# Dealing the units of an inner layer to partitions in runs of 7 and 9

## The chip, the cores and the metric

The kernel runs on one core of a Trainium2 chip. A core has five engines that run side by side, each with its own queue of instructions: TensorE (PE; its weight loads are listed apart as PEld), VectorE (DVE), ScalarE (ACT), GpSimd (POOL) and SyncE (SP, which only issues transfers here). Transfers between the large memory (HBM) and the on-chip memory (SBUF, 128 partitions) are done by 16 DMA engines. TensorE multiplies a stationary operand, which it loads first (LDWEIGHTS, at most 128 columns), with a moving operand and adds into the accumulator memory (PSUM). The metric is the device time of one execution in microseconds (us); where several runs are shown, their median.

## The reference

Two layers follow one another. The first is a short convolution along the sequence whose 7 taps differ for every token and head; the second is a two-matrix layer applied to each of the 32768 tokens.

```python
# x [8, 4096, 192], weight_gen [8, 4096, 8 heads, 7 taps]
w = exp(weight_gen - max) / sum over the taps
conv[b, s, h, g] = sum over k of w[b, s, h, k] * x_padded[b, s + k, h, g]   # 6 zero rows ahead
# w_in [192, 2048], w_out [2048, 192]
h = conv @ w_in
g = h - tanh(h)
out = g @ w_out            # [32768, 192], float32
```

The 2048 columns of `w_in` are the units of the inner layer. The output is a sum over units, so it doesn't matter in which order the units are taken, so long as column u of `w_in` and row u of `w_out` stay together.

## The kernel before

The tokens are cut into 32 tiles (`n`) of 1024, 8 neighbouring tokens to a partition. For each tile:

- SP loads the tile's `x` and tap weights. ScalarE takes the exponential; VectorE sums over the taps and divides.
- GpSimd, with help from VectorE, multiplies x with each tap's weight (`tap_product`, L303). Some of the seven products are added to each other by transfers that accumulate, issued by GpSimd (`dma_sum`, L292).
- TensorE turns the remaining products so that features lie on the partitions, and adds them up while it does so (`conv_sums`, L531: each product is the stationary operand, the identity the moving one). The 192 features are split as 64 x 3 with the 3 innermost, so a stationary operand there takes every third column. The 64 features of a group lie on the lower half of the partitions for one half of the tokens and on the upper half for the other. ScalarE copies the result to SBUF as `convT`.
- First matmul (`gemm1`, L591): for each of 16 blocks `f` of 128 units, three feature groups, and on both halves of the partitions at once: stationary `w_in` [64 features x 128 units], moving `convT` [64 x 512 tokens]. So six matmuls a block, which are three pairs, each pair on the two halves of the rows. `w_in` is kept twice for this, on the lower and on the upper 64 partitions.
- ScalarE takes tanh of the block's result (L604), VectorE subtracts (L605) and writes `gt`, bf16, with the 128 units of the block on the partitions.
- Second matmul (`out_stream`, L660): for each of 8 groups of 128 tokens, over the 16 blocks and the two halves of the units: stationary `gt` [64 units x 128 tokens], moving `w_out` [64 units x 192]. ScalarE copies the sums out (L679) and SP stores them.

The order of all this is written out by hand (`manual_schedule`). In tile n's turn the main loop goes over the 16 blocks: it issues `gemm1(n, f)` and then a number of steps of the second matmul of the tile before, read from a table (`pairs`, one number for each block; a zero means that the next block of the first matmul follows directly). The transposes of the next tile come behind blocks 13 and 14 in most turns. The last tile's second matmul is `last_rows` (L709).

Partition p of `w_out` in SBUF holds, for each block f, the row of the unit that the first matmul puts on partition p in block f. Before the change that is unit f*128 + p, since `gemm1` takes 128 adjacent columns of `w_in`. The weights are loaded once, at the start, by GpSimd, with a conversion from float32 to bf16: `w_in` in two parts, columns 0 to 895 (seven blocks, `FA = 7 * P`) and columns 896 to 2047 (nine blocks), both at L755; `w_out` in one transfer at L749, issued between GpSimd's tap products of tile 1. The upper copy of `w_in` is made by ScalarE for the first part (L822) and by a transfer on SP for the second (L830). The variant of the first matmul at `gemm1_relieved` is for blocks in the list `RELIEF`, which is empty.

Of the kernel before, what the change touches and what calls it, by code (L numbers as in the profile page):

```python
# [16 lines left out]
def kernel(  # L17
# [8 lines left out]
    nc = tc.nc  # L26
# [5 lines left out]
    P = nc.NUM_PARTITIONS  # L32
    R = P // 2
# [8 lines left out]
    NFT = F // P  # L42
# [214 lines left out]
    def softmax_norm_ramp(n, bank):  # L257

        softmax_sum(n)
        wsm = softmax_tile()  # L260
        zr_v = bank[:, 512 - J * H : 512]
        nc.vector.reciprocal(zr_v, zsum_of[n][:])  # L262
        if n == 2:
            scale(nc.vector, wsm[:], e_of[n], zr_v)
            wsm_of[n] = (wsm, None, None, None)
            return
        wsm_v = bank[:, 0 : J * H * K].rearrange("p (j h k) -> p j h k", j=J, h=H)
        if RAMP_TAPS is not None:
            for to_sbuf, k0, k1 in RAMP_TAPS[n]:
                ramp_scale[n] = scale(nc.vector, wsm[:] if to_sbuf else wsm_v, e_of[n], zr_v, k0, k1)  # L270
            wsm_of[n] = (wsm, wsm_v, None, None)
            return
        if n == 0 and SCALE_TWICE:
            scale(nc.vector, wsm[:], e_of[n], zr_v)
        ramp_scale[n] = scale(nc.vector, wsm_v, e_of[n], zr_v)
        if n == 1 or not SCALE_TWICE:
            nc.scalar.activation(
                out=wsm[:].rearrange("p j h k -> p (j h k)"),
                in_=wsm_v.rearrange("p j h k -> p (j h k)"),
                func=ACT.Copy,  # L280
            )
        wsm_of[n] = (wsm, wsm_v, None, None)
# [286 lines left out]
    def gemm1(n, f):  # L569
        convT = conv_of[n]  # L570
        ph = psum_h.tile([P, 2, HT], FP32, name="ph", tag="ph")
        ff = slice(f * P, (f + 1) * P)
        if n in THREE:
            block = convT[:].rearrange("p c (a t) -> p (c a) t", t=P).rearrange("p (j b) t -> p b j t", b=NC)
            for r, b, c, p0, p1, last in (
                (0, 0, 0, 0, P, False),
                (1, 2, 1, 0, P, False),
                (0, 1, 2, 0, R, True),
                (1, 1, 2, R, P, True),
            ):  # L580
                nc.tensor.matmul(
                    ph[:, r, :],
                    lhsT=w_nat_of[0][p0:p1, c, ff],
                    rhs=block[p0:p1, b],
                    start=not last,
                    stop=last,
                )
        else:
            for c in range(NC):
                for r in range(2):  # L590
                    nc.tensor.matmul(  # L591
                        ph[:, r, :],
                        lhsT=w_in[r * R : (r + 1) * R, c, ff],
                        rhs=convT[r * R : (r + 1) * R, c, :],
                        start=(c == 0),
                        stop=(c == NC - 1),
                    )
        th = tpool.tile([P, TOK], FP32, name="th")
        ph_f = ph[:].rearrange("p r t -> p (r t)")
        gt = gpool.tile([P, TOK], BF16, name=f"gt{f}", tag=f"gt{f}")  # L600
        if n == 1 and f == 2:

            probe[0] = nc.scalar.activation(out=once[:], in_=ph_f[:, 0:1], func=ACT.Copy)
        last_act[0] = nc.scalar.activation(out=th[:], in_=ph_f, func=ACT.Tanh)  # L604
        last_sub[0] = nc.vector.tensor_sub(gt[:], ph_f, th[:])  # L605
        if f == PACE:
            pace_of[n] = last_sub[0]
        g_of.setdefault(n, []).append(gt)
        return ph

    def gemm1_relieved(n, f):

        convT = conv_of[n]
        for c in range(NC):
            for r in range(2):
                nc.tensor.matmul(
                    obank[r][:],
                    lhsT=w_in[r * R : (r + 1) * R, c, f * P : (f + 1) * P],
                    rhs=convT[r * R : (r + 1) * R, c, :],
                    start=(c == 0),  # L620
                    stop=(c == NC - 1),
                )
        th = tpool.tile([P, TOK], FP32, name="th")
        gt = gpool.tile([P, TOK], BF16, name=f"gt{f}", tag=f"gt{f}")
        for r in range(2):
            nc.scalar.activation(out=th[:, r * HT : (r + 1) * HT], in_=obank[r][:], func=ACT.Tanh)
        g_of.setdefault(n, []).append(gt)

        def subtract():
            for r in range(2):  # L630
                nc.tensor.matmul(
                    obank[r][:], lhsT=minus[:], rhs=th[:, r * HT : (r + 1) * HT], start=False, stop=True
                )

        def evict():
            for r in range(2):
                nc.scalar.activation(out=gt[:, r * HT : (r + 1) * HT], in_=obank[r][:], func=ACT.Copy)

        return subtract, evict
# [59 lines left out]
    def last_rows(r):  # L699

        n = NTOT - 1
        for j in range(J):
# [5 lines left out]
            for f in range(NFT):  # L708
# [17 lines left out]
                        )  # L726
                yield

    w_in = const.tile([P, NC, F], BF16, name="w_in")
    w_out = const.tile([P, NFT, D], BF16, name="w_out")  # L730
    w_nat_of = {}
# [14 lines left out]
    ctx.enter_context(tc.manual_schedule())  # L746

    def load_w_out():
        nc.gpsimd.dma_start(out=w_out[:], in_=moe_w_out.rearrange("(c p) e -> p c e", c=NFT))  # L749

    FA = 7 * P

    def load_w_in(c0, c1, f0, f1, behind=None):
        src = moe_w_in[c0 : c0 + 1, f0:f1]
        dma = nc.gpsimd.dma_start(  # L755
            out=w_in[0:R, c0:c1, f0:f1],
            in_=bass.AP(
                tensor=src.tensor,
                offset=src.offset,
                ap=[[NC * F, R], [F, c1 - c0], [1, f1 - f0]],  # L760
            ),
        )
        if behind is not None:
            order(dma, behind, "order of the loads")

    def rest_of_w_in():
        load_w_in(0, NC, FA, F)

# [9 lines left out]
    for c0, c1 in W_CUTS:  # L778
        load_w_in(c0, c1, 0, FA, last_exp[0] if c0 == 0 else None)
    softmax_norm_ramp(0, obank[0])  # L780
# [36 lines left out]
    for c in range(NC + 1):  # L817
# [3 lines left out]
        if c < NC:  # L821
            nc.scalar.activation(out=w_in[R:P, c, 0:FA], in_=w_in[0:R, c, 0:FA], func=ACT.Copy)  # L822
    if SOFT_EARLY:
# [3 lines left out]
    if SOFT_EARLY:  # L827

        softmax_norm_ramp(2, obank[0])
    nc.sync.dma_start(out=w_in[R:P, :, FA:F], in_=w_in[0:R, :, FA:F])  # L830
    products(
# [21 lines left out]
    for f in range(NFT):  # L853
        if f in RELIEF:
            relieved = gemm1_relieved(0, f)
        else:
            helpers(0, f, gemm1(0, f))
# [65 lines left out]
    for n in range(1, NTOT):  # L923
# [5 lines left out]
        soft = [m for m in (n + 3 if n <= AHEAD else n + 4,) if m < NTOT]  # L929
        for f in range(NFT):  # L930
            ph = gemm1(n, f)
            if n == 1:
                if f == 1:
# [105 lines left out]
```

## Time and profile before

| | |
|---|---|
| runs | 736.35, 737.21, 737.90 us; median 737.21 |
| profiled execution | 735.98 us, span 734.2 us, granted TensorE clock 1.0 |
| busy in the span | PE 714.4 us, POOL 663.2, DVE 681.0, ACT 636.0, PEld 549.6 |
| weight loads of the first matmul | 3072, 94 ns each |
| weight loads of the second matmul | 7936 and 256, 94 ns each |
| issue of `w_in`, two parts (L755) | 0.79 and 0.67 us on GpSimd |
| issue of `w_out` (L749) | 1.20 us on GpSimd, at 23.75 us; landed 9.4 us later |

A line of a group reads: line of the kernel, engine, operation, output<-input, shapes, count | busy time, mean ns of one | idle time of the engine just before them and what ended it. A line of a timeline or of a chain reads: start in us, duration in us, what, with x for the number of instructions merged. A mean of one weight load is its time from issue to end; several overlap, so it isn't the time that the array needs for it.

### The profile page before, as it was taken

To read this page: it belongs to the slowest core of one execution; us is meant where nothing else is said; L and a number is where in the kernel's file an instruction comes from. 1 tells how busy PE (TensorE), PEld (TensorE's weight loads), DVE (VectorE), ACT (ScalarE), POOL (GpSimd) and SP (SyncE) were. 2 spreads that over 40 slices of the span, in tenths; PEclk is the share of its full clock that TensorE was granted. 3 is DMA by queue.
4 is the path that set the end of the run, shared out by engine and by line. 5 is a ranking of instruction groups with operands and counts; after the bars stand their busy time and mean duration, and the time that the engine had idled before them with its cause. 6 is when DMAs were issued, how large, how long until landed. Compare 5 with 4: busy or idle time off the path is not lost.

```text
span 734.2 us, 29608 instructions
## 1 busy us (share of the span) xinstructions
PE 714.4 (97%) x13376; PEld 549.6 (75%) x13376; DVE 681.0 (93%) x720; ACT 636.0 (87%) x871; POOL 663.2 (90%) x180
## 2 busy tenths in 40 slices
PE   3799999999999999999999999999999999999998
PEld 2477877778777777777777777777777777777777
DVE  7999999999999999999999999999999999988883
ACT  4888888888999898999898998988998989888982
POOL 7999999999999999999999999999999999996000
PEclk9999999999999999999999999999999999999999
DMA  7745266657778787877887878787877879676412
GB/s 206 162 102 163 101 167 166 175 131 186 170 175 217 155 220 183 181 200 174 211 174 205 203 157 208 163 206 188 216 166 176 209 159 222 163 153 137 104 46 88
DMA packets 35596, 124.53 MB, mean 170 GB/s; under 512 B 4639, under 2 KB 9487, under 8 KB 33550
## 3 DMA queue, kind: packets, MB, share of 16 engines
q0 software_dynamic: 20752, 55.05, 43.7%
q1 hardware_dynamic: 14718, 67.59, 25.8%
q8 instruction: 104, 1.70, 0.9%
q14 instruction: 22, 0.18, 0.1%
HBM read 45.08 MB, written 25.17 MB: 96 GB/s over the span
## 4 chain that ended last, share of the span: by engine, by line
PE 79%; POOL 11%; DVE 6%; DMA 2%; issue 1%; ACT 1%; POOLq 0%; DVEq 0%
PE obank L660 37%; PE ph L591 37%; POOL pa L303 5%; POOL pb L303 5%; DVE gt L605 3%; PE pc L531 3%; POOL pa L292 2%; PE po L709 1%; DMA pa<-pa 1%; DVE pa L303 1%; DVE pb L303 0%; DMA wg_t<-in_weight_gen_dram 0%; ACT th L604 0%; DVE zsum L222 0%; DVE obank L262 0%
## 5 line engine op out<-in xcount | busy, mean ns | idle before, releaser
L605 DVE TENSOR_TENSOR gt<-ph,th 128x1024 bf16<-128x1024 f32 x512 | 598.1, 1217 | 32.1 <-ACT th L604 25.8
L604 ACT ACTIVATE th<-ph 128x1024 f32<-128x1024 f32 x512 | 513.0, 1027 | 65.6 <-PE ph L591 51.1
L591 PE MATMUL ph<-convT,w_in 64*128 64x512 bf16 x3072 | 414.3, 378 | 4.5 <-DVE gt L605 3.5
L660 PEld LDWEIGHTS <-gt 64*128 64x128 bf16 x7936 | 353.7, 94 | 84.2 <-issue 12.6
L660 PE MATMUL obank<-w_out,gt 64*128 64x192 bf16 x7936 | 407.0, 243 | 0.1
L303 POOL TENSOR_TENSOR pa<-x_ring,wsm 128x3072 bf16<-128x3072 f32 (+4 forms) x81 | 357.0, 4775 | 0.2
L303 POOL TENSOR_TENSOR pb<-x_ring,wsm 128x4608 bf16<-128x4608 f32 (+4 forms) x34 | 290.9, 8556 | 1.0 <-DVE obank L285 1.0
L591 PEld LDWEIGHTS <-w_in 64*128 64x128 bf16 x3072 | 160.5, 94 | 79.4 <-issue 13.2
L679 ACT ACTIVATE out_sb<-obank 128x192 f32<-128x192 f32 x248 | 81.7, 329 | 9.6 <-PE obank L660 8.5
L292 POOL DMA_DIRECT2D pa<-pa x26 | 46.2, 1778 | 9.8 <-DMA pa<-pb 9.5
L557 ACT ACTIVATE convT<-pc 128x1024 bf16<-128x1024 f32 (+1 forms) x62 | 50.8, 821 | 3.8 <-PE pc L531 3.7
L292 POOL DMA_DIRECT2D pa<-pb x28 | 41.6, 1485 | 6.6 <-POOL pb L303 3.3
L531 PEld LDWEIGHTS <-pa 64*128 64x128 bf16 x1824 | 38.2, 101 | 7.6 <-issue 1.2
L531 PE MATMUL pc<-ident,pa 64*128 64x64 bf16 x1728 | 37.7, 193 | 2.1 <-DMA pa<-pa 0.8
L222 DVE TENSOR_REDUCE zsum<-wg_t 128x32 f32<-128x224 f32 (+1 forms) x61 | 23.6, 387 | 3.0 <-ACT wg_t L208 3.0
L208 ACT ACTIVATE wg_t<-wg_t 128x448 f32<-128x448 f32 x32 | 18.2, 569 | 6.5 <-DMA wg_t<-in_weight_gen_dram 6.5
L285 DVE TENSOR_TENSOR wsm<-wg_t,pc 128x448 f32<-128x448 f32 x27 | 16.8, 621 | 2.7
L303 DVE TENSOR_TENSOR pa<-x_ring,ph 128x384 bf16<-128x384 f32 x31 | 17.2, 554 | 1.3
L249 DVE RECIPROCAL pc<-zsum 128x64 f32<-128x64 f32 x27 | 14.8, 548 | 0.0
L531 PE MATMUL pc<-ident,pb 64*128 64x64 bf16 x216 | 4.9, 206 | 9.0 <-POOL pb L303 9.0
L531 PEld LDWEIGHTS <-pb 64*128 64x128 bf16 x288 | 6.3, 107 | 9.6 <-POOL pb L303 9.0
L709 PE MATMUL po<-w_out,gt 64*128 64x192 bf16 x256 | 11.9, 243 | 0.0
(26 smaller groups left out, 56.1 us busy)
## 6 DMA issues: line engine op xcount, KB each, us to landing
pa<-pb POOLq DMA_DIRECT2D x28, 1152.0 KB, 9.8
out_dram<-out_sb SPq DMA_DIRECT2D x31, 768.0 KB, 3.8
x_ring<-in_x_dram SPq DMA_DIRECT2D x15, 1344.0 KB, 7.5
pa<-pa POOLq DMA_DIRECT2D x26, 768.0 KB, 7.3
x_ring<-in_x_dram SPq DMA_DIRECT2D x17, 768.0 KB, 6.4
wg_t<-in_weight_gen_dram SPq DMA_DIRECT2D x32, 224.0 KB, 4.5
w_out<-in_moe_w_out_dram POOLq DMA_DIRECT2D x1, 768.0 KB, 9.4
out_dram<-out_sb SPq DMA_DIRECT2D x4, 192.0 KB, 1.9
```

The costliest lines, as they stand in the source:

```text
L208: last_exp[0] = nc.scalar.activation(out=wg_t[:].rearrange("p j h k -> p (j h k)"), in_=wg_t[:].rearrange("p j h k -> p (j h k)"), func=AC ...
L222: nc.vector.reduce_sum(out=zsum_of[n][:, j0 * H : j1 * H], in_=e_of[n][:, j0:j1].rearrange("p j h k -> p (j h) k"), axis=AX.X,)
L292: return nc.gpsimd.dma_start(out=out.rearrange("p k j d -> p k (j d)"), in_=in_.rearrange("p k j d -> p k (j d)"), accum_op=mybir.AluOpTyp ...
L303: return eng.tensor_mul(bass.AP(tensor=out.tensor, offset=out.offset + j0 * D, ap=[out.ap[0], [J * D, nk], [G, run], [1, G]]), bass.AP(ten ...
L531: nc.tensor.matmul(pc[r][:, col : col + R] if home else pc[:, r, col : col + R], lhsT=prods[c][gi][r * R : (r + 1) * R, 2 * j : 2 * j + 2] ...
L557: last_conv[0] = nc.scalar.activation(out=out, in_=pc[:, :, 0:cols].rearrange("p r (cj t) -> p r cj t", t=R), func=ACT.Copy,)
L591: nc.tensor.matmul(ph[:, r, :], lhsT=w_in[r * R : (r + 1) * R, c, ff], rhs=convT[r * R : (r + 1) * R, c, :], start=(c == 0), stop=(c == NC ...
L604: last_act[0] = nc.scalar.activation(out=th[:], in_=ph_f, func=ACT.Tanh)
L605: last_sub[0] = nc.vector.tensor_sub(gt[:], ph_f, th[:])
L660: mm = nc.tensor.matmul(po[:, 0:D], lhsT=g_of[n][f][r * R : (r + 1) * R, col : col + P], rhs=w_out[r * R : (r + 1) * R, f, :], start=(r == ...
L679: last_act[0] = nc.scalar.activation(out=out_sb[:, j, :], in_=po[:, 0:D], func=ACT.Copy)
L709: nc.tensor.matmul(po[:, r, 0:D], lhsT=g_of[n][f][r * R : (r + 1) * R, col : col + P], rhs=w_out[r * R : (r + 1) * R, f, :], start=(f == 0 ...
```

## The change

Units are dealt to blocks and partitions in another way. Inside the first 896 units, unit 7p + f goes to partition p of block f (f from 0 to 6); inside the other 1152, unit 896 + 9p + (f - 7) goes to partition p of block f (f from 7 to 15). So the rows of `w_out` that a partition holds are 7 neighbouring rows and 9 neighbouring rows of the matrix in HBM: one run of 7 x 768 bytes and one of 9 x 768 bytes, loaded by two transfers of 128 runs each in the place of one transfer of 2048 runs of 768 bytes. The stationary operand of the first matmul takes its 128 columns of `w_in` at a step of 7 elements for blocks 0 to 6 and of 9 elements for blocks 7 to 15, where the step was 1. The loads of `w_in` and everything behind the first matmul are as before.

```diff
                 for r in range(2):
                     nc.tensor.matmul(
                         ph[:, r, :],
-                        lhsT=w_in[r * R : (r + 1) * R, c, ff],
+                        lhsT=w_in[r * R : (r + 1) * R, c, hidden(f)],
                         rhs=convT[r * R : (r + 1) * R, c, :],
...
+    FA = 7 * P
+
+    def hidden(f):
+
+        f0, f1 = (0, FA // P) if f < FA // P else (FA // P, NFT)
+        return slice(f0 * P + f - f0, (f1 - 1) * P + P, f1 - f0)
+
...
     def load_w_out():
-        nc.gpsimd.dma_start(out=w_out[:], in_=moe_w_out.rearrange("(c p) e -> p c e", c=NFT))
-
-    FA = 7 * P
+        for f0, f1 in ((0, FA // P), (FA // P, NFT)):
+            nc.gpsimd.dma_start(
+                out=w_out[:, f0:f1], in_=moe_w_out[f0 * P : f1 * P].rearrange("(p c) e -> p c e", c=f1 - f0)
+            )
```

The same replacement of the column slice stands in `gemm1_relieved`, which is not run.

More of the change, by code (lines that the diff above doesn't have):

```diff
@@ L617, in gemm1_relieved @@
                     obank[r][:],
-                    lhsT=w_in[r * R : (r + 1) * R, c, f * P : (f + 1) * P],
+                    lhsT=w_in[r * R : (r + 1) * R, c, hidden(f)],
                     rhs=convT[r * R : (r + 1) * R, c, :],
```

## The prediction

> **What bounds the kernel now.** I read the page's busy shares first, then the chain that ended last, then the groups by line, then the chain piece by piece, then the start of the kernel in order of time. The changed lines touch two engines: TensorE, whose weight loads of the first matmul change their pattern, and GpSimd, which issues the load of the output weights.
>
> The page, busy shares and the chain by engine and line:
>
> ```profile
> PE 714.4 (97%) x13376; PEld 549.6 (75%) x13376; DVE 681.0 (93%) x720; ACT 636.0 (87%) x871; POOL 663.2 (90%) x180
> ...
> PE 79%; POOL 11%; DVE 6%; DMA 2%; issue 1%; ACT 1%; POOLq 0%; DVEq 0%
> ```
>
> The reader sees that TensorE carries the end nearly alone, that GpSimd carries a stretch, and that weight loads (PEld) are busy but are not themselves in the chain: they run beside matmuls. The groups by line:
>
> ```profile
> L591 PE MATMUL ph<-convT,w_in 64*128 64x512 bf16 x3072 | 414.3, 378 | 4.5 <-DVE gt L605 3.5
> ...
> L591 PEld LDWEIGHTS <-w_in 64*128 64x128 bf16 x3072 | 160.5, 94 | 79.4 <-issue 13.2
> ...
> L531 PEld LDWEIGHTS <-pa 64*128 64x128 bf16 x1824 | 38.2, 101 | 7.6 <-issue 1.2
> ```
>
> The middle line is what the change alters: 3072 loads of 128 adjacent columns, 94 ns each. The last line is the only strided load of this kernel: the transposes at L531 take every third column (the feature index is split with c innermost, three values), 6 bytes apart, and are recorded with 101 ns. The chain piece by piece, columns start, duration, what:
>
> ```profile
> 166.04 0.29 PE obank L660 x6
> 166.32 0.94 PE pc L531 x64
> ...
> 414.71 0.65 PE ph L591 x6
> ```
>
> Matmuls go in pairs, one on each half of the rows. A pair of the first matmul (L591) takes 0.65/3 = 216 ns, a pair of the second (L660) 82 ns in the start times, a pair of transposes 0.94/32 = 29 ns. The load for a pair is issued about 2 ns after the pair before it starts; so the pair before is its cover: 216, 82 or 29 ns. Since the transposes run at 29 ns a pair, a load at a step of 6 bytes occupies its half of the array for no more than 29 ns, whatever its recorded 101 ns of latency. The start of the kernel on GpSimd, in order of time:
>
> ```profile
> 14.63 0.67 POOL L755 DMA_DIRECT2D w_in<-in_moe_w_in_dram  x1
> 15.32 8.48 POOL L303 TENSOR_TENSOR pb<-x_ring,wsm 128x3072 bf16<-128x3072 f32 x2
> 23.75 1.20 POOL L749 DMA_DIRECT2D w_out<-in_moe_w_out_dram  x1
> 24.98 16.78 POOL L303 TENSOR_TENSOR pa<-x_ring,wsm 128x3072 bf16<-128x3072 f32 x3
> ```
>
> GpSimd stands on the issue of w_out for 1.20 us with its tap products queued behind it. From here on it is busy without a gap worth naming until 270 us (the stretch from 180 to 280 us shows 100.00 of 100 us busy), and one place hands its time to TensorE, the wait for its last sum in the table of waits:
>
> ```profile
> PE pc L531 <- DMA pa<-pa: 0.8, 1, 0.8
> ```
>
> After that wait, at 279.35 us, TensorE is busy for 437 of 437 us to 717. So time lost on GpSimd before 270 us comes out at the end about one to one; time won comes out only up to 0.8 us.
>
> **Weight loads of the first matmul.** Same 3072 loads, same 128 columns; the columns now lie 7 elements (14 bytes) apart for units 0 to 6 and 9 elements (18 bytes) for units 7 to 15. No view shows such a step. In order of start, 399 of the 512 units begin behind a pair of the second matmul (cover 82 ns; 237 of them units 7 to 15), 31 behind transposes (cover 29 ns; 30 of them units 7 to 15), 82 behind another unit (216 ns). Loads inside a unit have 216 ns. With an occupancy t, the cost is 31 x (t - 29) + 399 x (t - 82), each where positive.
> Lower end: t stays at the strided row's 29 ns or less: 0. A gain is excluded, since a load that is hidden already can give nothing. Upper end: t grows with the bytes spanned, three times the span of a step of 3 for a step of 9: 87 ns, which gives 31 x 58 + 237 x 5 = 1.8 + 1.2 = 3.0 us. I take the lower end. Contiguous 94 and strided 101 ns differ by 7 ns for a threefold span, so latency goes up far slower than the span: the same 7 ns again for each further threefold, or twice that, leaves t under 45 ns, worth at most 31 x 16 = 0.5 us. Cover gone altogether is the first rival below.
>
> [...]
>
> **The load of w_out.** Removed: one issue of 2048 runs (1536 KB read, 768 KB written, 384 bytes a run), 1.20 us at L749. Added: two issues of 128 runs each, of 2688 and 3456 bytes written. The nearest row is L755 (192 runs): 0.67 and 0.79 us. Two at 0.67 and 0.03 us between are 1.37, so GpSimd loses 1.37 - 1.20 = 0.17 us. Ends: each costs as much as the old one, +1.2 us; or the cost goes with the runs, 1.20 x 256/2048 = 0.15 in all, -1.05 us, of which 0.8 can come out. I take +0.15, by L755, which has nearly the same number of runs.
> The transfer itself: the packets of w_out run from 27.9 to 32.3 us, 768 KB in 4.4 us; those of the second part of w_in (2304 bytes written) from 16.6 to 19.1, 432 KB in 2.5 us. That is 175 and 173 KB/us: no difference by the size of the run, so again about 4.4 us. [...]
> Landing was 9.4 us after issue, at 33.2; the first second-matmul starts at 37.89. It now waits for two transfers instead of one, ahead of everything TensorE has queued, with 4.7 us to spare: 0.
> What does move is the start. The old load's first packet came 4.1 us after its issue, the one of w_in 2.0 us after: with few runs it should begin at about 25.7, while SP's load of x for the third tile (1344 KB, issued 20.68, landed 7.5 us later at 28.2) is still running. GpSimd needs that x at 30.56. At 25.7 the x load has 2.45 us to go; sharing the engines half and half it lands at 30.6, and with larger packets than w_out's (10752 bytes) somewhat earlier. So it stays hidden, by little: 0, upper end 1.8 us (w_out wholly first: 28.2 + 4.4 = 32.6, against 30.56 + 0.17).
>
> SP's queue issues nothing new and nothing is moved past it; the copies of w_in to the upper partitions keep their columns. The branch at L618 is not run, its list of units is empty.
>
> **Sum.** 0 (loads) + 0.15 (issues) + 0 (transfer) = +0.15 us on the profiled execution, which took 735.98 us (span 734.2 and 1.8 around it): 736.1. That execution lies 1.2 us under the median of the runs, 737.21, so as a median 737.4.
>
> **The rivals.** About 0.2%, 1.5 us, is what runs of this kernel (736.35 to 737.9) can tell from no change.
> *Wide loads lose their cover* (slower). Place: the first pair of a unit. It decides from t = 82 ns; below that only the 31 places behind transposes pay. At four times the strided row, t = 116: 31 x 87 + 399 x 34 = 2.7 + 13.6 = 16.3 us, 753.7. For it: no row has so wide a step. Against: 7 ns for the step of 3. Chance 0.18.
> [...] Chance of more than 1.5 us: 0.10. [...]
> *The earlier w_out takes the place of x* (slower). GpSimd waits at 30.56 for up to 1.8 us, its tap products are queued behind, and the 0.8 us wait at 279 grows by that: 737.4 + 1.8 = 739.2. It decides when x lands later than 30.7. For it: both transfers fill the engines. Against: the half-and-half estimate still fits. Chance 0.10.
> *Fewer runs pay off* (faster). The issues shrink to 0.15 us, the 0.8 us wait at 279 goes, and the 0.77 us in which TensorE stands before its last transpose at 32.14, waiting for nothing that the profile names, goes too, if w_out's packets, in flight at that time, were its cause: 737.2 - 1.6 = 735.6. Chance 0.10. With it, "one run in memory" would do what it says.
> *Forecast:* no change, 0.52, its own range 736.2 to 738.7.
>
> **The numbers.** Faster 0.10, same 0.52, slower 0.18 + 0.10 + 0.10 = 0.38. The time is that of the forecast, 737.4. The range goes from 736.2 (leaving out most of the faster case) up to 750, past the collision and the step of 9 and half of the wide-load case; about 2 in 10 stay outside.
>
> **What would show it.** Right: L591's loads at 95 to 125 ns, pairs still 82 ns apart where a unit follows the second matmul; two L749 issues of about 0.67 us; x landing before 30.7 us. [...]

## The result and the profile after

The change makes the kernel slower: 743.84 us median of 6 runs against 736.94 us of 6 runs before, a ratio of 1.0094 with a 95% interval of 1.0078 to 1.0110. The profiled execution took 742.63 us (span 740.9), 6.65 us more than the one before. The time lies inside the stated range and on the side that had a chance of 0.38, but none of the rivals named what happened.

The page of the changed kernel, busy shares and the chain by engine:

```profile
PE 717.4 (97%) x13376; PEld 604.8 (82%) x13376; DVE 682.2 (92%) x720; ACT 636.4 (86%) x871; POOL 663.2 (90%) x181
...
PE 94%; DMA 2%; DVE 1%; ACT 1%; issue 1%; POOL 1%; SPq 0%; POOLq 0%; DVEq 0%
```

GpSimd has gone from the chain (11% to 1%), TensorE carries it from start to end, and weight loads are busy for 55 us more. The groups of the first matmul and its loads:

```profile
L591 PE MATMUL ph<-convT,w_in 64*128 64x512 bf16 x3072 | 420.6, 379 | 9.6 <-DMA w_in<-w_in 3.6
...
L591 PEld LDWEIGHTS <-w_in 64*128 64x128 bf16 x3072 | 212.1, 133 | 54.4 <-issue 10.8
```

Two things are new. The mean load took 133 ns instead of 94. And the idle time before the matmuls has a releaser that the kernel before didn't show: the copy of `w_in` to the upper partitions. When that was is in the timeline of TensorE around the first tile (start, duration, what, and in brackets the idle time before and its releaser), after the change:

```profile
16.62 0.64 PE L591 MATMUL ph<-convT,w_in 64*128 64x512 bf16 x2 [0.90 <-ACT convT L557]
20.11 0.63 PE L591 MATMUL ph<-convT,w_in 64*128 64x512 bf16 x1 [2.85 <-DMA w_in<-in_moe_w_in_dram]
24.30 3.19 PE L591 MATMUL ph<-convT,w_in 64*128 64x512 bf16 x14 [3.55 <-DMA w_in<-w_in]
```

and before it:

```profile
16.46 4.03 PE L591 MATMUL ph<-convT,w_in 64*128 64x512 bf16 x18 [0.90 <-ACT convT L557]
21.59 0.82 PE L591 MATMUL ph<-convT,w_in 64*128 64x512 bf16 x6 [1.10 <-DVE gt L605]
```

Before, 18 matmuls (three blocks) start without a break at 16.46. After, the first pair runs (feature group 0), the third matmul (group 1, lower partitions) stands until GpSimd's second load of `w_in` has landed, and the fourth (group 1, upper partitions) until SP's copy of that second part has landed, at 24.3. Block 0 reads from the first 896 columns of each feature group; both transfers write the other 1152. So it waits for data that it doesn't use.

Setting the start of a tile's first matmul beside that of the kernel before divides the loss (worked out from the start times in the two traces):

| start of | later than before by | what happened up to there |
|---|---|---|
| second block of tile 0 | 7.0 us | the two waits |
| tile 1 | 6.2 us | 0.8 of the 7.0 is won back in the first tile, where TensorE waits for VectorE's `gt` (3.5 us in all before, 2.1 after) |
| tile 11 | 6.65 us | the wider loads, and small shifts |
| tile 12 | 5.8 us | TensorE's wait of 0.8 us for its last accumulating transfer at 279 us is gone, since TensorE is now the later one |
| tile 30 | 6.63 us | from tile 13 on 0.77 us are added, 45 ns a tile |

### The profile page after: what moved, and what is told of

Read it like the earlier page. It is cut to its first block, busy times and chain, and to the rows that moved or that the text cites. A ratio compares the mean times of both kernels' runs of the same rounds, so it can differ in the third digit from the quotient of the medians.

```text
span 740.9 us, 29609 instructions
## 1 busy us (share of the span) xinstructions
PE 717.4 (97%) x13376; PEld 604.8 (82%) x13376; DVE 682.2 (92%) x720; ACT 636.4 (86%) x871; POOL 663.2 (90%) x181
## 4 chain that ended last, share of the span: by engine, by line
PE 94%; DMA 2%; DVE 1%; ACT 1%; issue 1%; POOL 1%; SPq 0%; POOLq 0%; DVEq 0%
PE obank L660 44%; PE ph L591 44%; PE pc L531 4%; PE po L709 1%; DVE gt L605 1%; DMA x_ring<-zero 1%; DMA w_in<-in_moe_w_in_dram 1%; POOL pa L303 1%; DMA w_in<-w_in 1%; ACT th L604 0%; SPq L178 0%; ACT wg_t L208 0%; ACT convT L549 0%; SPq L167 0%; DVE out_sb L720 0%
## 5 line engine op out<-in xcount | busy, mean ns | idle before, releaser
L591 PE MATMUL ph<-convT,w_in 64*128 64x512 bf16 x3072 | 420.6, 379 | 9.6 <-DMA w_in<-w_in 3.6
L660 PEld LDWEIGHTS <-gt 64*128 64x128 bf16 x7936 | 358.1, 94 | 63.9 <-issue 10.6
L591 PEld LDWEIGHTS <-w_in 64*128 64x128 bf16 x3072 | 212.1, 133 | 54.4 <-issue 10.8
L531 PEld LDWEIGHTS <-pa 64*128 64x128 bf16 x1824 | 39.4, 101 | 4.5 <-POOL pa L303 1.1
L531 PE MATMUL pc<-ident,pa 64*128 64x64 bf16 x1728 | 37.8, 193 | 1.3 <-POOL pa L303 0.9
L531 PEld LDWEIGHTS <-pb 64*128 64x128 bf16 x288 | 6.6, 107 | 9.5 <-POOL pb L303 9.2
L531 PE MATMUL pc<-ident,pb 64*128 64x64 bf16 x216 | 5.0, 206 | 9.2 <-POOL pb L303 9.2
```

Of the source, the lines that this page charges most:

```text
L531: nc.tensor.matmul(pc[r][:, col : col + R] if home else pc[:, r, col : col + R], lhsT=prods[c][gi][r * R : (r + 1) * R, 2 * j : 2 * j + 2] ...
L591: nc.tensor.matmul(ph[:, r, :], lhsT=w_in[r * R : (r + 1) * R, c, hidden(f)], rhs=convT[r * R : (r + 1) * R, c, :], start=(c == 0), stop=( ...
L660: mm = nc.tensor.matmul(po[:, 0:D], lhsT=g_of[n][f][r * R : (r + 1) * R, col : col + P], rhs=w_out[r * R : (r + 1) * R, f, :], start=(r == ...
```

## The experiments

Theory A: the loss is a wait. In the first tile, the slice with a step is ordered behind transfers that it doesn't read. Theory B: the loss is spread over the run, in weight loads of 133 instead of 94 ns. The kernel before was run again beside each of three groups of runs. Its medians were 736.4 us beside the first-tile, later-tiles, wait-alone and two-tiles runs, 736.15 beside the control, the load alone and the wider steps, and 736.25 beside the layout part by part. Each ratio is to the runs of its own group.

**Stepped columns in the first tile only.**

```diff
-                        lhsT=w_in[r * R : (r + 1) * R, c, hidden(f)],
+                        lhsT=w_in[r * R : (r + 1) * R, c, hidden(f) if n == 0 else ff],
```

> The change, with stepped columns in the first tile only; tiles 1 to 31 take 128 adjacent columns, so that for these tiles the units don't match the rows of w_out and the output isn't the reference's. Theory A: nearly the whole loss stays, +6.2 us at the first unit, less 0.8 to 0.9 us that a wait at 279 us gives back: 742 to 742.8. Theory B: 31 of 32 of the loss go, 737.2.

Measured: 742.73 us, ratio 1.0081 (1.0064 to 1.0098). One tile of 32 holds nearly all of the loss. The waits of TensorE are the same two:

```profile
PE ph L591 <- DMA w_in<-w_in: 3.6, 1, 3.6
...
PE ph L591 <- DMA w_in<-in_moe_w_in_dram: 2.9, 1, 2.9
```

**Stepped columns in all tiles but the first.**

```diff
+                        lhsT=w_in[r * R : (r + 1) * R, c, hidden(f) if n > 0 else ff],
```

> The counterpart: adjacent columns in the first tile, stepped ones in tiles 1 to 31 (the first tile's units don't match the rows of w_out). Theory A: the wait at the start goes; what is left is the price of the loads alone, about 45 ns for each of 31 tiles, 1.4 us: 738 to 738.6. Theory B: 743.6.

Measured: 737.58 us, ratio 1.0009 (1.0000 to 1.0018), a little under the 738 that was expected. The loads are as long as in the change, and no wait on a transfer of `w_in` is left:

```profile
L591 PEld LDWEIGHTS <-w_in 64*128 64x128 bf16 x3072 | 210.6, 132 | 49.7 <-issue 12.2
```

Loads of 132 ns in 31 tiles cost about a microsecond, not seven. Theory B falls.

**The wait without any step.** The kernel before, with one added order:

```diff
-                    nc.tensor.matmul(
+                    mm = nc.tensor.matmul(
...
+                    if (n, f, c, r) == (0, 0, 1, 1):
+                        order(mm, upper[0], "place of the first unit")
...
+    upper[0] = nc.sync.dma_start(out=w_in[R:P, :, FA:F], in_=w_in[0:R, :, FA:F])
```

> The kernel before the change, with one wait added: the fourth matmul of the first block of the first tile waits for the copy of the second part of w_in to the upper partitions (landed at 24.1 us). No stepped column anywhere; the output is the reference's. Theory A: this alone gives the loss of the first tile, 742 to 742.8 us. Theory B: the start has slack, below 739.

Measured: 742.47 us, ratio 1.0078 (1.0063 to 1.0093), as theory A has it. Its timeline (one line has been added above, so L591 is L592 here):

```profile
16.82 0.71 PE L592 MATMUL ph<-convT,w_in 64*128 64x512 bf16 x3 [1.00 <-ACT convT L558]
24.66 2.74 PE L592 MATMUL ph<-convT,w_in 64*128 64x512 bf16 x12 [7.13 <-DMA w_in<-w_in]
```

A wait of 7.13 us at the start came out as 6.0 us at the end (742.47 against 736.44 beside it). The change lost 6.9 us against its own runs of the kernel before, so about 0.9 us is left for the stepped loads, by a difference of medians.

**The two parts of `w_in` as two tiles.**

```diff
-    w_in = const.tile([P, NC, F], BF16, name="w_in")
+    w_in = [const.tile([P, NC, n], BF16, name=f"w_in{i}") for i, n in enumerate((7 * P, F - 7 * P))]
...
+                        lhsT=w_in[f >= FA // P][r * R : (r + 1) * R, c, hidden(f)],
```

> The change, with w_in kept as two tiles in SBUF (the first 896 columns, the other 1152), columns at steps of 7 and 9 as in the change; the output is the reference's. Theory A (the loss is a wait: in the first tile the stepped columns of blocks 0 to 6 are ordered behind the load and the copy of the other 1152 columns, which they don't read): the two waits of L591 on DMA, 2.9 and 3.6 us, go, the second unit starts near 17.8 us as before the change, and the time is 737 to 739 us (before, 736.9, plus about 45 ns a tile for the wider loads). Theory B (the loss is spread over the run, in weight loads of 133 instead of 94 ns): no change from 743.8.

Measured: 737.56 us, ratio 1.0010 (1.0000 to 1.0019). The same steps, the same loads, and no wait on a transfer: TensorE's idle time before L591 is

```profile
PE ph L591 <- DVE gt L605: 2.4, 6, 1.0
PE ph L591 <- ACT convT L557: 0.9, 1, 0.9
```

**Its control: two tiles, adjacent columns, `w_out` loaded as before.**

> The kernel before the change with w_in as two tiles, columns adjacent, w_out loaded as before: the control for the two tiles. Both theories: as before the change, 736 to 738 us.

Measured: 736.34 us, ratio 0.9999 (0.9989 to 1.0008). The two tiles by themselves cost nothing.

**One tile, laid out part by part.** Nothing so far says why a stepped slice is ordered in this way. Here `w_in` is one tile again, but holds the first 896 columns of all three feature groups and behind them the other 1152 of all three:

```diff
+    w_in = const.tile([P, NC * F], BF16, name="w_in")
+
+    def part(f0, f1):
+
+        return w_in[:, NC * f0 : NC * f1].rearrange("p (c f) -> p c f", c=NC)
```

> The change with w_in as one tile again, but its columns laid out part by part: the first 896 columns of all three feature groups, then the other 1152 of all three; steps 7 and 9, the output is the reference's. If the order of a stepped slice is worked out from the stretch of memory from its first to its last element (in the change, the stretch of the second and third feature group lies between the first and the last byte of the other part's load): the stretches no longer cross, the two waits of L591 on DMA go, 737 to 738.5 us. If it goes by the whole tile: 743 to 744.5, with the waits.

Measured: 737.64 us, ratio 1.0018 (1.0007 to 1.0030). The waits are gone:

```profile
16.54 3.68 PE L591 MATMUL ph<-convT,w_in 64*128 64x512 bf16 x18 [1.00 <-ACT convT L557]
21.62 0.86 PE L591 MATMUL ph<-convT,w_in 64*128 64x512 bf16 x6 [1.40 <-DVE gt L605]
```

No line of the kernel asks for the two waits; the author's inference is a comparison of the memory that a matmul reads with the memory that an earlier transfer writes. The result fits a comparison by stretches for slices with a step. In the change's layout, the second part's load writes columns 896 to 2047 of every feature group, and its stretch, from first to last byte of a partition, includes the first 896 columns of groups 1 and 2, but not those of group 0. By it group 0 could run at 16.62 and group 1 couldn't. An order by the whole tile is ruled out, by group 0 and by this run. With adjacent columns the same three-group load had made nobody wait (18 matmuls without a break from 16.46), so a slice without a step wasn't held to the load's stretch. The rule itself is inferred from these runs; how the comparison is made isn't shown.

**The load of `w_out` alone**, with adjacent columns in all tiles.

> The change's two transfers for w_out alone, with adjacent columns of w_in in all tiles (units and rows of w_out don't match, the output isn't the reference's). Theory A and B: 736.5 to 737.5, GpSimd's time for both issues 1.15 instead of 1.20 us. Rival from the prediction, the earlier transfer takes the place of x: up to 739, with GpSimd idle at 30.6 us.

Measured: 735.98 us, ratio 0.9998 (0.9988 to 1.0007). What the change is named after makes no difference that can be measured. GpSimd in its timeline:

```profile
24.21 1.15 POOL L757 DMA_DIRECT2D w_out<-in_moe_w_out_dram  x2
25.37 11.21 POOL L303 TENSOR_TENSOR pa<-x_ring,wsm 128x3072 bf16<-128x3072 f32 x2
```

Two issues in 1.15 us, against 1.20 for the single one, and the products behind go on without a gap. The 0.77 us in which TensorE stood at 32.14 us before the change is gone in this run, but in the control with the old load too, and neither is faster by more than its interval.

**Wider steps, tiles 1 to 31.** All blocks at a step of 16 or 48 columns:

```diff
+                        lhsT=w_in[r * R : (r + 1) * R, c, slice(f, F, 16) if n > 0 else ff],
```

> As the run with stepped columns after the first tile, with a step of 16 columns (32 bytes) in all blocks of tiles 1 to 31; the output isn't the reference's. If the load's time goes with the bytes spanned: 29 x 16/3 = 155 ns, over the cover of 82 ns at about 387 places and of 29 ns at 30: + 28 + 4 = 32 us, 769. [...]

> The same with a step of 48 columns (96 bytes). With the bytes spanned: 464 ns, over every cover, more than 900 us. [...]

Measured: 737.41 us, ratio 1.0015 (1.0005 to 1.0024), with 16; 737.68 us, ratio 1.0018 (1.0009 to 1.0028), with 48. The loads, with a step of 16 and, in the second fence, of 48:

```profile
L591 PEld LDWEIGHTS <-w_in 64*128 64x128 bf16 x3072 | 221.6, 141 | 43.2 <-issue 10.7
```

```profile
L591 PEld LDWEIGHTS <-w_in 64*128 64x128 bf16 x3072 | 225.9, 143 | 41.3 <-issue 11.3
```

Neither comes near the time of a load that goes with the bytes spanned, 769 us with 16 and more than 900 with 48. A load's time hardly grows: from 16 to 48 the span triples and 2 ns are added (141 to 143). (With 48 the start of tile 7 also slips by 0.6 us once, which the run with 16 doesn't show.)

**Where the 45 ns of a tile arise.** The start times in the traces before and after, block 10 of tile 14, matmuls of the upper half of the rows, in ns from the start of the block before:

```
                      first matmul   its next load   next matmul
before                     1020           1031           1246
after                      1010           1044           1278
```

The block's first pair had waited for its PSUM buffer: VectorE's subtraction ended at 959 (before) and 951 (after). The lower half's load had been issued at 895, during the pair before, but the upper half's only with the wait's end, at 1016 and 1006. That half's first matmul is then recorded with 427 ns instead of 387, and its next matmul comes 42 ns later relative to it (268 ns instead of 226 apart). The delay stays until the end of the tile and adds up over tiles.

Elsewhere the first pair of a block follows the pair ahead of it as before the change, 82 to 83 ns behind a pair of the second matmul and 29 ns behind transposes. In block 15, which stands behind the transposes, its loads are issued only 28 ns ahead of their matmuls, and the block's second pair comes 245 ns after the first instead of 217 (medians of tiles 13 to 30). Those 28 ns are made up again by the pairs behind: at the start of the next tile the median of what is left is 0.

No run was faster than the kernel before by more than its interval, and the parts show why: the new load of `w_out` gains nothing, the stepped columns cost 1.1 to 1.4 us without the wait and 6.9 with it.

## Why the prediction was right and wrong

- **The sum, +0.15 us, was wrong**, by 6.5 us on the profiled execution. The step that failed stands in the part on the weight loads: it took from the edit only that the columns lie further apart, and asked how long a load takes. It didn't ask what a slice with a step is ordered behind. The prediction looked for added waits at the load of `w_out` and at SP's queue and found none to matter; the one that decided was at the first matmul's reads of a tile that is still being written. The rows for it were all there: the second load of `w_in` issued at 14.63 us, the copy issued at 19.91, and the first block started at 16.46, between them. So was the price: the copy landed at 24.1, 7.6 us after the first block's start. The runs showed in its place a delay of 7.0 us at the second block. With the two parts kept apart 5.5 to 5.8 of the 6.9 us lost go, and the 1.1 to 1.4 us that stay are the loads'.
- **Chances.** Slower had 0.38 for three mechanisms, wide loads, the step of 9 alone and a collision with x. None took place: the loss belongs to a fourth. That the step of 9 alone pays, 0.10 of the 0.38, is a term that no run shows: the median load took 134 ns at 9 against 128 at 7, and the pairs behind the second matmul stood 82 to 83 ns apart in the change as before it. The forecast's own range, 736.2 to 738.7, was missed by 5.1 us. That the time fell into the full range (736.2 to 750) is luck, owed to the width that the rivals gave it.
- **Loads hidden: right in the main, with one term missed.** The cover of 82 ns held in all runs (pairs 82 to 83 ns apart). Behind transposes the cover of 29 ns did not: 28 ns showed at block 15 (median of tiles 13 to 30), where the prediction allowed at most 16 from an occupancy under 45 ns, and they cost nothing in the end only because the pairs behind made them up. The loads' latency went to a median of 128 ns at a step of 7 and 134 at 9, above the 125 that the prediction allowed. The missed term is the block whose first pair waits for a PSUM buffer, where the second load isn't issued ahead: 45 ns a tile, about 1.4 us in all, where the sum had 0.
- **The rivals of wide loads fell.** At a step of 48 the pairs behind the second matmul still stood 82 to 83 ns apart. The step of 9 doesn't stand apart from 7 either: 134 against 128 ns. Of the 40 ns by which a load at a step of 9 outlasts one of adjacent columns (94), 34 were there at 7; what makes it so isn't shown.
- **Issue of `w_out`:** +0.17 us forecast, -0.05 measured (1.15 against 1.20). The two issues took 0.61 and 0.55 us, less than the nearest row of 0.67. Transfer and landing made nobody wait, as said.
- **The earlier start of w_out, wrong.** It was to begin at about 25.7 us and crowd x. Its first packet is recorded at 27.7 us, as against 27.5 before the change (the 27.9 of the prediction was read too late), when x had nearly landed; x landed 7.4 us after its issue as against 7.5, and GpSimd didn't wait for it. So the late start isn't a matter of the number of runs. In all eleven traces the first packet came 3.4 to 3.9 us after the issue and at most 0.4 us before the last packet of x ended, whereas the second part of `w_in` began 1.4 us after its issue. That looks like a transfer that starts when x is nearly through, but no run tests it. That two transfers share the engines half and half was the author's estimate, which isn't shown either.
- **The equal rates, misread.** The prediction took the packets of `w_out` from 27.9 to 32.3 us and those of `w_in` from 16.6 to 19.1. In the packet records they run from 27.5 to 32.9 and from 16.0 to 19.6, 143 and 121 KB/us from end to end. So the agreement of 175 and 173 isn't shown, and neither is what the prediction concluded from it. Over the middle four fifths of its bytes, `w_out` moved at 183 to 187 KB/us in the three traces with pieces of 384 written bytes and at 199 to 211 in the eight with pieces of 2688 and 3456. The longer pieces were somewhat faster, and nobody waited for them.
- **The 0.8 us at 279 us** did come out: it was given back when TensorE became the later one, in the change and in the run with the wait alone (with steps in the first tile only, half of that wait was still there, 0.4 us).
- **"One run in memory" brings a gain:** no. Alone it gave a ratio of 0.9998 (0.9988 to 1.0007).

## What to carry to other kernels

An edit of an access pattern is also an edit of the order: while a tile is still being filled, ask for every slice that reads it which of the writes in flight its stretch crosses. Parts that are loaded at different times belong in tiles, or at least in stretches, of their own; here the loss went from 6.9 us to 1.1 with two tiles and to 1.4 with one tile laid out part by part. Before making a transfer's runs longer, look whether anyone waits for it: nobody waited for `w_out`.

## What the hardware showed

- Weight loads of 128 columns of bf16 on 64 partitions took 94 ns with adjacent columns, 101 at a step of 3 (`pa`, L531), 128 at 7 and 134 at 9 (medians), 141 at 16 and 143 at 48 (means). Issued about 81 ns ahead of its matmul, during a pair of the second matmul, no load was seen in the pairs' distance (82 to 83 ns), not even at a step of 48.
- Loads that were issued less far ahead did show. In the first matmul's pairs at a step of 9, the next pair came 28 ns later than with adjacent columns where the loads were issued 28 ns ahead, and 42 ns later where one was issued about 5 ns ahead (tile 14, block 10); the median load at that step took 40 ns longer.
- Loads from HBM with conversion to bf16 moved at 183 to 187 KB/us in pieces of 384 written bytes and at 199 to 211 in pieces of 2688 and 3456 (middle four fifths of the bytes of `w_out`; other transfers partly in flight). The issue on GpSimd cost 1.20 us for 2048 runs, 0.67 to 0.79 for 192 and 0.55 to 0.61 for 128.
